# Three-token rows, PE turns for the first two blocks and a fixed instruction list in a chunked-attention plus gated-FFN kernel

## The chip, the cores and the metric

One core of one Trainium2 chip. The metric is device time in microseconds (us) of one execution. The kernel before takes 298.7 us (median of 3 runs, 298.63 to 300.44). The profile shows the span from the first to the last instruction; in every execution of which both are listed, the time is 1.7 to 2.4 us above the span. PE is TensorE (PEld its weight loads), DVE is VectorE, ACT is ScalarE, POOL is GpSimd, SP is SyncE, which issues most of the DMAs.

## The reference

Inputs are q, k, v of shape [4, 8, 768, 64], 8 memory rows per head, and three FFN weights of 512x1536, 512x1536 and 1536x512, all float32.

```python
for c in range(nc):                              # chunks of 32 queries
    l_start, r_end = max(0, 32*c - 16), min(S, 32*c + 40)
    k_full = concat([mem_k, k[:, :, l_start:r_end]], axis=2)   # v_full likewise
    scores = scale * q_c @ k_full.T
    out[chunk] = softmax(scores) @ v_full
x = out.transpose(0, 2, 1, 3).reshape(3072, 512)
y = (maximum(x @ w_gate, 0) * (x @ w_val)) @ w_out
```

## The kernel before

It works in 8 blocks of 384 tokens. A block is 4 attention steps of 96 queries (against 120 keys and 8 memory rows), 12 FFN units (four gate and four value matmuls each) and 3 output units of 12 matmuls. Attention needs q and k with the head dimension on partitions, the FFN needs the attention output x with features on partitions. All of this turning is done by DMA transposes, issued by SP.

```python
# loads: one token per partition and head, so 256 B runs
def src(self, t, h0, nh, tok, parts):
    return bass.AP(tensor=t.tensor, offset=t[self.b, h0, tok, 0].offset,
                   ap=[[D, parts], [S * D, nh], [1, D]])
...
def cast_q(self, h0, nh):            # two zero-padded copies of q, one per head of a pair
    for x in range(2):
        nc.vector.tensor_copy(self.qn[:, p0:p1, x, :, D * x:D * x + D], view[:, x])
def turn_q(self, h0, nh):
    nc.sync.dma_start_transpose(self.qT[:, p0:p1]..., self.qn[:, p0:p1]...)
...
# scores of 4 heads: two matmuls of 192 columns over 128 rows
nc.tensor.matmul(s_ps[:, i], lhsT=blk.kb[:, 2 * g + i, j, :], rhs=blk.qT[...], start=True, stop=True)
...
# start: block 0, then weights, then block 1
for h0 in (0, 4):
    b0.load_k(h0, 4, sp); b0.load_q(h0, 4, nc.scalar.dma_start); b0.load_v(h0, 4, sp)
nc.gpsimd.tensor_copy(gate, b0.qf[:, 0, 4, 0:1])
...                                  # 9 weight loads on POOL's queue, 1 MB read each
for h in range(2):
    b0.cast_k(4 * h, 4); b0.turn_k(4 * h, 4); b0.cast_q(4 * h, 4); b0.turn_q(4 * h, 4)
    b0.cast_v(4 * h, 4); b0.bands(4 * h, 4)
    if h == 0:
        load_all(blocks[1])
    ...                              # scores and values of block 0
```

The order of the program is not the order on the engines here: the framework's scheduler rearranges it.

The softmax here doesn't subtract the row's maximum and nothing guards it: scores larger than these inputs give would overflow.

Of the kernel before, what the change touches and what calls it, by code (L numbers as in the profile page):

```python
# [7 lines left out]
F32 = mybir.dt.float32  # L8
F16 = mybir.dt.float16
BF16 = mybir.dt.bfloat16  # L10
# [6 lines left out]
def kernel(  # L17
# [30 lines left out]
    KCOLS = 512  # L48
    MEMCOL = 400

    wpool = ctx.enter_context(tc.tile_pool(name="wpool", bufs=1))
    vpool = ctx.enter_context(tc.tile_pool(name="vpool", bufs=2))
    tpool = ctx.enter_context(tc.tile_pool(name="tpool", bufs=2))
    rpool = ctx.enter_context(tc.tile_pool(name="rpool", bufs=4))
    xpool = ctx.enter_context(tc.tile_pool(name="xpool", bufs=6))
# [3 lines left out]
    opool = ctx.enter_context(tc.tile_pool(name="opool", bufs=3))  # L59

    sps = ctx.enter_context(tc.tile_pool(name="sps", bufs=2, space=bass.MemoryType.PSUM))
    pps = ctx.enter_context(tc.tile_pool(name="pps", bufs=1, space=bass.MemoryType.PSUM))
    fps = ctx.enter_context(tc.tile_pool(name="fps", bufs=4, space=bass.MemoryType.PSUM))
    ops = ctx.enter_context(tc.tile_pool(name="ops", bufs=1, space=bass.MemoryType.PSUM))



    qn_t = [wpool.tile([128, HP, 2, NT, 2 * D], BF16, name=f"qn{i}") for i in range(2)]
    kf_t = [wpool.tile([128, 4, H, D], F32, name=f"kf{i}") for i in range(2)]
    vb_t = [wpool.tile([128, NJ, H, VW], F16, name=f"vb{i}") for i in range(3)]  # L70
    vf_t = [wpool.tile([128, NJ, H, D], F32, name=f"vf{i}") for i in range(2)]
    memv = wpool.tile([NMEM, B * H, D], F32, name="memv")
    ex_t = [wpool.tile([128, 4, 128], F16, name=f"ex{i}") for i in range(3)]
    for i in range(2):
        nc.vector.memset(kf_t[i][:, 3], 0.0)
    for i in range(2):
        nc.vector.memset(qn_t[i], 0.0)
    for t in vf_t:
        nc.gpsimd.memset(t[0:NMEM], 0.0)
    for t in ex_t:  # L80
        nc.gpsimd.memset(t[:, :, QB:128], 0.0)
    for t in vb_t:
        nc.gpsimd.memset(t[:, :, :, D:VW], 1.0)
# [3 lines left out]

    def build_mask(name, qb):

        m = wpool.tile([128, QB], F16, name=name)  # L90
        nc.gpsimd.memset(m, 1.0)
        bs = q_band_start(qb) - NMEM
        for g in range(QB // 32):
            c = 3 * qb + g
            lo = max(32 * c - 16, 0) - bs
            hi = min(32 * c + 40, S) - bs
            sl = m[:, 32 * g:32 * g + 32]
            if lo > NMEM:
                nc.gpsimd.affine_select(
                    out=sl, in_=sl, pattern=[[0, 32]], compare_op=ALU.is_ge,  # L100
                    fill=0.0, base=-lo, channel_multiplier=1,
                )
            if hi < 128:
                nc.gpsimd.affine_select(
                    out=sl, in_=sl, pattern=[[0, 32]], compare_op=ALU.is_ge,
                    fill=0.0, base=hi - 1, channel_multiplier=-1,
                )
        nc.gpsimd.memset(m[0:NMEM], 1.0)
        return m

    masks = {}

    def mask_of(qb):
        return masks["first" if qb == 0 else ("last" if qb == NQB - 1 else "int")]

    w_gate_sb = wpool.tile([128, NFC, DFF], F16, name="w_gate_sb")
    w_val_sb = wpool.tile([128, NFC, DFF], F16, name="w_val_sb")
    w_out_sb = wpool.tile([128, NDC, DM], F16, name="w_out_sb")

    class Block:  # L120


        def __init__(self, n):
            self.n, self.b, self.T = n, n // 2, n % 2
            self.kbase = 0 if self.T == 0 else MB - 16
            self.starts = [q_band_start(NJ * self.T + j) for j in range(NJ)]
            self.qn, self.kf = qn_t[n % 2], kf_t[n % 2]
            self.vb = vb_t[n % 3]
            self.qf = vpool.tile([128, NT, H, D], F32, name="qf")
            self.vf = vf_t[n % 2]  # L130
            self.kn = vpool.tile([128, HP, 4, 2 * D], BF16, name="kn")
            self.qT = tpool.tile([128, HP, 2, NT, 128], BF16, name="qT")
            self.kT = tpool.tile([128, HP, KCOLS], BF16, name="kT")
            self.kb = tpool.tile([128, HP, NJ, 128], BF16, name="kb")
            self.xT = None

        def src(self, t, h0, nh, tok, parts):
            return bass.AP(
                tensor=t.tensor, offset=t[self.b, h0, tok, 0].offset,
                ap=[[D, parts], [S * D, nh], [1, D]],  # L140
            )

        def load_k(self, h0, nh, dma):
            hs = slice(h0, h0 + nh)
            for t in range(3):
                dma(self.kf[:, t, hs, :], self.src(k, h0, nh, self.kbase + 128 * t, 128))  # L146
            dma(self.kf[0:16, 3, hs, :], self.src(k, h0, nh, self.kbase + 384, 16))
            dma(self.kf[16:24, 3, hs, :], bass.AP(
                tensor=mem_k.tensor, offset=mem_k[self.b, h0, 0, 0].offset,
                ap=[[D, NMEM], [NMEM * D, nh], [1, D]]))  # L150

        def load_q(self, h0, nh, dma):
            hs = slice(h0, h0 + nh)
            for t in range(NT):
                dma(self.qf[:, t, hs, :], self.src(q, h0, nh, MB * self.T + 128 * t, 128))

        def load_v(self, h0, nh, dma):
            hs = slice(h0, h0 + nh)
            for j in range(NJ):
                dma(self.vf[NMEM:128, j, hs, :], self.src(v, h0, nh, self.starts[j], BAND))  # L160

        def cast_k(self, h0, nh):
            p0, p1 = h0 // 2, (h0 + nh) // 2
            nc.vector.tensor_copy(
                self.kn[:, p0:p1], self.kf[:, :, h0:h0 + nh, :].rearrange("p t (a x) d -> p a t (x d)", x=2))

        def cast_q(self, h0, nh):
            p0, p1 = h0 // 2, (h0 + nh) // 2
            view = self.qf[:, :, h0:h0 + nh, :].rearrange("p t (a x) d -> p x a t d", x=2)
            for x in range(2):  # L170
                nc.vector.tensor_copy(self.qn[:, p0:p1, x, :, D * x:D * x + D], view[:, x])

        def cast_v(self, h0, nh):
            nc.vector.tensor_copy(self.vb[:, :, h0:h0 + nh, 0:D], self.vf[:, :, h0:h0 + nh, :])  # L174
            m = memv[:, H * self.b + h0:H * self.b + h0 + nh, :]
            m4 = bass.AP(tensor=m.tensor, offset=m.offset, ap=[m.ap[0], [0, NJ], [D, nh], [1, D]])
            nc.gpsimd.tensor_copy(self.vb[0:NMEM, :, h0:h0 + nh, 0:D], m4)  # L177

        def turn_k(self, h0, nh):
            p0, p1 = h0 // 2, (h0 + nh) // 2  # L180
            nc.sync.dma_start_transpose(  # L181
                self.kT[:, p0:p1].rearrange("p a (t c) -> p (a t) c", c=128),
                self.kn[:, p0:p1].rearrange("p a t c -> p (a t c)"))

        def turn_q(self, h0, nh):
            p0, p1 = h0 // 2, (h0 + nh) // 2
            nc.sync.dma_start_transpose(  # L187
                self.qT[:, p0:p1].rearrange("p a x t c -> p (a x t) c"),
                self.qn[:, p0:p1].rearrange("p a x t c -> p (a x t c)"))

        def bands(self, h0, nh):
            p0, np_ = h0 // 2, nh // 2
            kT, kb = self.kT, self.kb

            def band(off, mids, n):
                return bass.AP(tensor=kT.tensor, offset=kT.offset + KCOLS * p0 + off,
                               ap=[kT.ap[0], [KCOLS, np_]] + mids + [[1, n]])
            rel = [s - self.kbase for s in self.starts]
            odd = 0 if self.T == 0 else NJ - 1
            first = 1 if self.T == 0 else 0  # L200
            nc.vector.tensor_copy(kb[:, p0:p0 + np_, first:first + 3, NMEM:128],  # L201
                                  band(rel[first], [[QB, 3]], BAND))
            nc.vector.tensor_copy(kb[:, p0:p0 + np_, odd, NMEM:128], band(rel[odd], [], BAND))
            nc.vector.tensor_copy(kb[:, p0:p0 + np_, :, 0:NMEM],  # L204
                                  band(MEMCOL, [[0, NJ]], NMEM))

    n_exp = [0]

    def quad_stages(blk, j, g, x_big):
        st = {}  # L210

        def scores():
            s_ps = sps.tile([128, 2, 2, QB], F32, name="s_ps")
            for i in range(2):
                nc.tensor.matmul(  # L215
# [106 lines left out]
    for h in range(2):  # L322
# [6 lines left out]
        if h == 0:  # L329
            load_all(blocks[1])  # L330
# [61 lines left out]
```

## Time and profile before

| stretch (us) | what happens | what limits |
|---|---|---|
| 0 to 72.2 | q, k, v of blocks 0 and 1, all weights, DMA transposes, attention of blocks 0 and 1 | DMA: share 1.1 to 1.3 of 16 engines, at 176 to 198 GB/s |
| 72.2 to 290.4 | FFN of 8 blocks, attention of the next block between | PE: busy 209 of 218 us |
| 290.4 to 294.4 | last copy and store | tail |

The table of stretches of the kernel before has, for each stretch, the busy time (and instructions) of each engine, the granted clock, the DMA share and what the DMA engines moved:

```profile
core 0: us, PE busy (x) PEld busy (x) DVE busy (x) ACT busy (x) POOL busy (x), PEclk, DMA share, GB/s
0.00:22.00 22.00, 0.00 (x0) 0.00 (x0) 7.39 (x11) 1.28 (x1) 16.88 (x41) 1.00 1.11 193
22.00:45.00 23.00, 0.22 (x2) 0.32 (x3) 1.26 (x4) 0.00 (x0) 1.52 (x4) 1.00 1.27 176
45.00:72.20 27.20, 9.85 (x76) 6.22 (x75) 16.83 (x46) 6.56 (x14) 1.93 (x1) 1.00 1.09 198
```

For 45 us PE and ACT do next to nothing (POOL's 16.9 us go mostly to clearing buffers, building masks, casts and issuing weight loads), and the DMA engines are full. (The profile prints shares above 1; read them as full.) They move only 176 to 198 GB/s. The page's lines on packets and queues point to a reason, which e1 below tests:

```profile
DMA packets 146152, 45.82 MB, mean 156 GB/s; under 512 B 138436, under 2 KB 143044, under 8 KB 146132
...
q0 software_dynamic: 4800, 4.79, 9.7%
q10 hardware_dynamic: 3168, 0.79, 1.5%
```

95% of the packets are under 512 B. Queue q10 holds nothing but such packets: 1.5% of 16 engines' 294.4 us over 3168 packets is 22 ns each, or about 180 GB/s for all 16 engines. Queue q0, 9.7% of the engines' time or 28.6 us of all 16, is nearly all weights.

SP's queue shows what stands behind this traffic. Its timeline in the start (start, duration, queue, line, operation):

```profile
15.88 9.64 SPq L181 DMA_TRANSPOSE kT<-kn  x1
25.62 9.75 SPq L187 DMA_TRANSPOSE qT<-qn_94  x1
35.43 8.93 SPq L146 DMA_DIRECT2D kf_97<-in_k_dram  x3
```

The first two transposes hold SP for almost 20 us while weights and loads fill the engines, and the loads of block 1 are issued only after them. The list of PE's waits has the total, the count and the longest:

```profile
PE s_ps L215 <- DMA qT<-qn_94: 47.6, 3, 44.8
PE o_ps L231 <- DVE x_big L236: 10.7, 6, 7.4
PE s_ps L215 <- DMA qT<-qn_95: 4.6, 2, 3.8
```

The 44.8 us is the start. The other 7.4 us of waits for qT (2.8 and 4.6) lie in later blocks: PE is nearly full there, but not quite.

### The profile page before, as it was taken

What the parts mean: (1) busy time and instruction counts of PE and PEld (TensorE: products, weight loads), DVE (VectorE), ACT (ScalarE), POOL (GpSimd) and SP (SyncE); (2) the same over time, 40 slices, a digit from 0 to 9 for tenths busy, and PEclk for the clock granted to TensorE, in tenths of its full rate; (3) what the DMA queues carried; (4) which work ended last, traced back from release to release, by engine and by line L of the source; (5) the groups of instructions that cost most, each with busy time, mean ns of one, the idle gap of its engine ahead of it and who ended that gap; (6) DMA issues with size and microseconds to landing.
All of it is one profiled execution on the core that took longest, in us unless ns stands there. A gap on an engine that the chain in (4) does not pass through costs nothing.

```text
span 294.4 us, 4093 instructions
## 1 busy us (share of the span) xinstructions
PE 219.2 (74%) x1440; PEld 123.4 (42%) x1440; DVE 140.4 (48%) x355; ACT 92.9 (32%) x185; POOL 31.7 (11%) x52
## 2 busy tenths in 40 slices
PE   0000002147999799989999999999999499999983
PEld 0000001024554266546545654664565256545641
DVE  4400103675584079429924971884398127612310
ACT  1000002023342165236424622642453136423411
POOL 7950200020002000200020020002002000000000
PEclk9999999999999799999999999999999999999999
DMA  9999999997929877899499989969896611111001
GB/s 166 217 197 187 195 145 207 233 181 168 218 51 171 207 163 157 135 243 239 92 205 246 217 121 237 225 136 193 223 245 119 139 71 28 29 51 59 0 36 71
DMA packets 146152, 45.82 MB, mean 156 GB/s; under 512 B 138436, under 2 KB 143044, under 8 KB 146132
## 3 DMA queue, kind: packets, MB, share of 16 engines
q1 hardware_dynamic: 138164, 39.99, 67.1%
q0 software_dynamic: 4800, 4.79, 9.7%
q10 hardware_dynamic: 3168, 0.79, 1.5%
q8 instruction: 11, 0.18, 0.2%
q14 instruction: 9, 0.07, 0.1%
HBM read 30.34 MB, written 6.29 MB: 124 GB/s over the span
## 4 chain that ended last, share of the span: by engine, by line
PE 62%; DMA 21%; SPq 8%; DVE 5%; issue 1%; ACT 1%; ACTq 0%; DVEq 0%
PE vl_ps L273 20%; PE g_ps L269 19%; PE out_ps L284 16%; DMA vf_101<-in_v_dram 5%; DMA qT<-qn_94 5%; DMA qT<-qn_95 5%; PE o_ps L231 4%; PE s_ps L215 4%; DMA qf<-in_q_dram 3%; SPq L146 3%; DMA kf_96<-in_k_dram 2%; SPq L187 2%; SPq L181 1%; DVE gvT L277 1%; DMA xT<-x_big 1%
## 5 line engine op out<-in xcount | busy, mean ns | idle before, releaser
L269 PE MATMUL g_ps<-xT,w_gate_sb 128*128 128x384 f16 x384 | 81.9, 328 | 0.4 <-DMA xT<-x_big 0.4
L273 PE MATMUL vl_ps<-xT,w_val_sb 128*128 128x384 f16 x384 | 80.1, 329 | 0.0
L277 DVE TENSOR_TENSOR gvT<-vl_ps,g_relu 128x384 f16<-128x384 f32 x96 | 53.3, 555 | 54.3 <-PE vl_ps L273 53.0
L284 PE MATMUL out_ps<-w_out_sb,gvT 128*128 128x512 f16 x288 | 67.5, 385 | 1.6 <-ACT o_sb L287 1.3
L215 PE MATMUL s_ps<-qT,kb 128*128 128x192 bf16 x128 | 23.1, 272 | 58.4 <-DMA qT<-qn_94 47.6
L276 ACT ACTIVATE g_relu<-g_ps 128x384 f16<-128x384 f32 x96 | 47.2, 492 | 49.0 <-PE g_ps L269 31.9
L273 PEld LDWEIGHTS <-w_val_sb 128*128 128x128 f16 x384 | 37.6, 98 | 24.6 <-issue 0.7
L284 PEld LDWEIGHTS <-gvT 128*128 128x128 f16 x288 | 28.5, 99 | 36.4 <-issue 6.6
L269 PEld LDWEIGHTS <-w_gate_sb 128*128 128x128 f16 x384 | 35.7, 98 | 18.8 <-issue 1.6
L215 PEld LDWEIGHTS <-kb 128*128 128x128 bf16 x128 | 11.6, 105 | 64.4 <-DVE kb L204 40.8
L287 ACT COPY o_sb<-out_ps 128x512 f32<-128x512 f32 x24 | 14.1, 587 | 63.1 <-PE out_ps L284 63.1
L236 DVE TENSOR_TENSOR x_big<-o_ps,rinv 96x256 f16<-96x256 f32 x64 | 26.7, 418 | 1.2
L222 ACT ACTIVATE ex_104<-s_ps 128x384 f16<-128x384 f32 x22 | 10.8, 493 | 46.0 <-PE s_ps L215 44.6
L222 ACT ACTIVATE ex_105<-s_ps 128x384 f16<-128x384 f32 x21 | 10.3, 492 | 21.8 <-PE s_ps L215 20.9
L222 ACT ACTIVATE ex_106<-s_ps 128x384 f16<-128x384 f32 x21 | 10.3, 492 | 12.6 <-PE s_ps L215 11.9
L177 POOL CAST vb_99<-memv 8x2048 f16<-8x2048 f32 x3 | 5.7, 1903 | 75.9 <-DVE vb_99 L174 75.9
L177 POOL CAST vb_98<-memv 8x1024 f16<-8x1024 f32 (+1 forms) x4 | 5.8, 1458 | 64.0 <-DVE vb_98 L174 64.0
L234 DVE RECIPROCAL rinv<-o_ps 96x4 f32<-96x4 f32 x64 | 11.0, 171 | 3.2 <-PE o_ps L231 2.9
L201 DVE COPY kb<-kT 128x1440 bf16<-128x1440 bf16 (+1 forms) x9 | 4.8, 531 | 15.6 <-DMA kT<-kn 15.6
L174 DVE CAST vb_98<-vf_101 128x1024 f16<-128x1024 f32 (+1 forms) x3 | 2.6, 868 | 15.9 <-DMA vf_101<-in_v_dram 15.9
L231 PEld LDWEIGHTS <-ex_105 128*128 128x128 f16 x84 | 4.9, 103 | 11.9 <-DVE x_big L236 10.5
L177 POOL CAST vb_100<-memv 8x2048 f16<-8x2048 f32 x2 | 3.8, 1886 | 54.1 <-DVE vb_100 L174 54.1
(65 smaller groups left out, 107.6 us busy)
## 6 DMA issues: line engine op xcount, KB each, us to landing
out_dram<-o_sb SPq DMA_DIRECT2D x24, 256.0 KB
qf<-in_q_dram SPq DMA_DIRECT2D x21, 256.0 KB
vf_102<-in_v_dram SPq DMA_DIRECT2D x16, 240.0 KB
kf_97<-in_k_dram SPq DMA_DIRECT2D x12, 256.0 KB
vf_101<-in_v_dram SPq DMA_DIRECT2D x12, 240.0 KB
kf_96<-in_k_dram SPq DMA_DIRECT2D x9, 256.0 KB
w_gate_sb<-in_moe_w_gate_dram POOLq DMA_DIRECT2D x3, 512.0 KB, 10.3
w_val_sb<-in_moe_w_val_dram POOLq DMA_DIRECT2D x3, 512.0 KB, 12.7
```

Of the source, the lines that this page charges most:

```text
L177: nc.gpsimd.tensor_copy(self.vb[0:NMEM, :, h0:h0 + nh, 0:D], m4)
L215: nc.tensor.matmul(s_ps[:, i], lhsT=blk.kb[:, 2 * g + i, j, :], rhs=blk.qT[:, 2 * g + i].rearrange("p x t c -> p x (t c)")[:, :, QB * j:QB ...
L222: nc.scalar.activation(e, s_ps.rearrange("p a x c -> p (a x) c"), ACT.Exp, scale=SCALE)
L231: nc.tensor.matmul(o_ps[:, i, :], lhsT=st["ex"][:, i, :], rhs=blk.vb[:, j, 4 * g + i, :], start=True, stop=True)
L234: nc.vector.reciprocal(rinv, o_ps[0:QB, :, D:D + 1])
L236: nc.vector.tensor_tensor(out=x_big[:, 256 * g:256 * g + 256].rearrange("p (h d) -> p h d", h=4), in0=o_ps[0:QB, :, 0:D], in1=rinv_b, op=A ...
L269: nc.tensor.matmul(g_ps, lhsT=w_gate_sb[:, f, 128 * m:128 * m + 128], rhs=blk.xT[:, f, :], start=(f == 0), stop=(f == NFC - 1))
L273: nc.tensor.matmul(vl_ps, lhsT=w_val_sb[:, f, 128 * m:128 * m + 128], rhs=blk.xT[:, f, :], start=(f == 0), stop=(f == NFC - 1))
L276: nc.scalar.activation(g_relu, g_ps, ACT.Relu)
L277: nc.vector.tensor_tensor(out=state["gvT"][:, m, :], in0=vl_ps, in1=g_relu, op=ALU.mult)
L284: nc.tensor.matmul(out_ps, lhsT=state["gvT"][:, m, 128 * t:128 * t + 128], rhs=w_out_sb[:, m, :], start=(m == 0), stop=(m == NDC - 1))
L287: nc.scalar.copy(o_sb, out_ps)
```

## The change

Its intent is to get PE to the FFN sooner. For all blocks q and k, and for blocks 0 and 1 also v, are loaded with three neighbouring tokens per partition, so that a run is 768 B. Blocks 0 and 1 use no DMA transpose at all: PE turns q, k and x, and sorts keys and values into bands by matmuls with step matrices. Their instructions stand in one fixed list, and the framework's scheduler is switched off. The weight loads are spread out: POOL issues them in groups, where the kernel before issues all of them from 7.4 us on. Blocks 2 to 7 still turn by DMA, but without the zero-padded q: scores are computed on 64 rows per head. Exp runs over 8 heads at once, and the value matmuls of attention stand between an FFN unit's gate and value matmuls.

```diff
+    ctx.enter_context(tc.manual_schedule())
...
+    def load3(eng, c, n, h0=0, nh=H):
+        src = bass.AP(tensor=t.tensor, offset=t[n // 2, h0, MB * i, 0].offset,
+                      ap=[[R3 * D, 128], [S * D, nh], [1, R3 * D]])
+        eng.dma_start(dst, src)
...
+            for a in range(HP):
+                for x in range(2):
+                    r = slice(D * x, D * x + D)
...
+                        pe.matmul(o.rearrange("p (t c) -> p t c", t=R3), lhsT=self.kb[r, a, j, :],
+                                  rhs=qT_t[i][r, a, :, PP * j:PP * j + PP], start=True, stop=True)
...
+        def turn_pe(self):
+            for f in range(NFC):
+                pe.transpose(self.t16[:, f], self.x[:, 128 * f:128 * f + 128], id16[0:QB, 0:QB])
...
+    def dff(n, m, mid=()):
+        g = relu(dff_mm(n, w_gate_sb, m))
+        for f in mid:
+            f()
+        product(n, m, dff_mm(n, w_val_sb, m), g)
...
+    def gather_v(n, j):
+        mm = [(step3[:, s0 - MB * i - t:s0 - MB * i - t + BAND], v16[:, i, :, t, :]) for t in range(R3)]
...
+        for e, (w, r) in enumerate(mm):
+            pe.matmul(o[0:BAND], lhsT=w, rhs=r, start=(e == 0), stop=(e == len(mm) - 1))
...
+    def keep(n):                       # filler matmuls on zeros
+        for _ in range(n):
+            pe.matmul(PS[:, 3, 4 * VW:512], lhsT=zero[:, 0:128], rhs=zero[:, 0:512 - 4 * VW], start=True, stop=True)
...
+    load3(sp, "k", 1)
+    keep(20)
+    ORDER = """
+        kx16:A ck00:D mlast:P key0 ck01:D cq00:P key0e:A key2 key2e:A cq01:D d2 key3 vm16:D key3e:A d3 q01 q01e:A
...
+        T0 q10 kt0 kt0e:D S3 e0:A q10e:A b0:D P2 T1 x3:A M3 wb:P bm:D G4 e1:A S4 n2:D P3 bi2:D T2 G5 g4:A bi0:D
+        x4:A wc:P bi1:D n3:D S5 b3:P S6 g5:D e2:A T3 M4 P4 G6 x5:A S7 e3:D x6:A n4:D g6:A M5 M6:D fg01 P5 T4 n5:D
...
+    """.split()
...
+        elif nm == "vm16":
+            eng(vm16[:, :, :, 0:D], ...)
+            sp.dma_start(vb_t[0][BAND:128], vm16)
+            load3(sp, "q", 1)
+            load3(sp, "v", 1)
+            sp.dma_start(vb_t[1][BAND:128], vm16)
```

In the list S is scores, x exp, P value matmuls, n normalisation, T the turn of x and e its eviction, G and g the gathering of v, fg and fv gate and value matmuls of an FFN unit; the letter after the colon is the engine.

## The prediction

> **What bounds the kernel now.** Two stretches. (1) Start: in the timeline the first gate matmul runs at 72.2 us; until then PE is nearly idle, while the slice table shows the DMA engines full at only 145 to 233 GB/s. The table of queues explains the rate: nearly all packets are under 512 B (256 B rows of q, k, v), and a 250 B packet cost about 22 ns of an engine (1.5% of 16 engines' 294 us over 3168 packets), about 180 GB/s for all 16. The DMA transposes stand behind those loads: in the waits the first score matmul waits 44.8 us, for qT. (2) From 72.2 to 290.4 us PE is the limit: busy 209 of 218 us in the table of stretches. A middle block takes 26.2 us: 96 gate/value matmuls of 162 ns (four take 0.65 us in the chain), 36 output matmuls of 216 ns, together 23.4, and about 2.8 us of attention. About 9 us are PE waits, mostly for qT (pieces of 6 to 8 us in the chain). A tail of 4 us follows; the measured time is 4.3 us above the span.
>
> **What the change does.** Rows of three tokens make packets of 768 B. The Trainium skill ("DMA: Bandwidth & Descriptors", Specifications) puts line rate at 512 B and up; this trace has no 768 B packets, but its 2 KB output packets moved at about 320 GB/s (35 GB/s at a share of 0.11). I estimate 250 to 300 GB/s. Blocks 0 and 1 no longer need DMA transposes. For later blocks the zero-padded q goes (half of q's transposed bytes). PE gains about 20 us of work at the start (gathers, turns, masks), where it idled.
>
> Start, estimated: q, k, v of block 0 land by about 11 us, of block 1 by about 20. Then VectorE (about 24 us: evictions at 0.65, normalisations at 0.9, products 0.555) and ScalarE (about 22 us: exps of 768 columns at 0.78, from 492 and 587 ns; copies 0.5 to 0.6, relus 0.49) set the pace. The first FFN matmuls come at 24 to 28 us, the first eight FFN units (10.4 us of PE) are done at about 36. Then weights limit for a while: all weights cost 27 us of DMA (9.7% of the span), three blocks of q, k, v and the transposes about 33, so w_out is complete at 62 to 66 us, where a free PE would want it at 57. I put this stall, partly seen as ScalarE standing at the casts of block 2, at 5 us.
>
> Steady: 8 blocks of 23.4 = 187; attention on 6 blocks only. Scores on 64-row halves can run two at a time, saving about 0.6 us a block; the skill's "TensorEngine Tiling (Array Packing)", Key Properties, says that a mode switch drains the array, and no run shows it yet, so 2.4 us a block: 14. Small gaps 3. DMA share falls well below 0.9, so the qT waits go.
>
> Sum: FFN work as if dense from 27, stall 5, 187 + 14 + 3, tail 4 = 240 span, + 4.3: **244 us, 234 to 257**. Faster by over 2%: 0.97; within 2%: 0.02; slower: 0.01.
>
> **Right or wrong, in the profile.** First gate matmul at 24 to 28 us; packets down by more than half; steady block 25.8 us or less with no PE wait on qT; first output matmul at 62 to 66 us; PE gaps between 30 and 65 us ended by weights or block 2's loads.
>
> **What would make it wrong.** 768 B packets no better than 200 GB/s; the fixed order jamming in-order engines, so that the start passes 45 us; POOL's slow descriptor writing delaying weights; drains of a microsecond per step; or no stall at all (then 236).

## The result and the profile after

The kernel after takes 246.55 us (median of 4 runs, 245.21 to 247.25), the kernel before 298.66 beside it. The ratio is 0.8244, with a 95% interval of 0.8208 to 0.8279. A ratio here is always the mean time of one kernel's fast runs over that of the kernel before in the same rounds, so it is not quite the ratio of the medians quoted. The profiled execution has a span of 244.6 us and a granted clock of 0.996; it was a run of 246.31 us.

The stretches of the kernel after, in the same columns as above:

```profile
0.00:22.00 22.00, 17.65 (x161) 11.32 (x162) 11.29 (x27) 10.84 (x16) 14.06 (x40) 1.00 0.94 245
22.00:38.00 16.00, 14.71 (x182) 9.54 (x181) 10.24 (x26) 10.45 (x19) 8.21 (x14) 1.00 0.97 163
38.00:67.30 29.30, 29.06 (x222) 17.14 (x220) 16.32 (x32) 15.17 (x29) 6.77 (x12) 1.00 1.06 181
```

PE, idle for 45 us before, is now busy nearly from the beginning (its first 5 us are filler). From 22 us on it is busy 14.7 of 16 us, then 29.1 of 29.3 us. The packet lines of the page after:

```profile
DMA packets 84414, 39.46 MB, mean 161 GB/s; under 512 B 57112, under 2 KB 81432, under 8 KB 84392
```

Packets fell by 42%, not by more than half: v of blocks 2 to 7 is still loaded in rows of 256 B (by the shapes of these loads about 23,000 of the 57,112 small packets that are left). PE's timeline gives the milestones:

```profile
30.23 0.82 PE L307 MATMUL PS<-xT,w_gate_sb 128*128 128x384 f16 x4
...
43.85 0.81 PE L307 MATMUL PS<-xT,w_gate_sb 128*128 128x384 f16 x4
...
67.26 1.89 PE L334 MATMUL PS<-w_out_sb,gvT 128*128 128x512 f16 x8
69.69 1.02 PE L334 MATMUL PS<-w_out_sb,gvT 128*128 128x512 f16 x4 [0.55 <-DMA w_out_sb<-in_moe_w_out_dram]
...
84.82 0.81 PE L307 MATMUL PS<-xT,w_gate_sb 128*128 128x384 f16 x4 [0.90 <-DMA xT<-x_big]
...
87.77 0.81 PE L307 MATMUL PS<-xT,w_val_sb 128*128 128x384 f16 x4 [0.84 <-ACT o_sb L348]
```

The first gate matmul runs at 30.2 us instead of 72.2: 42 of the span's 49.8 us. The remaining 8 us are about the size of the 7.4 us of qT waits in later blocks, and PE's list of waits no longer has a wait for qT at all; no run separates the parts of these 8 us. At 43.85 us the first eight FFN units (64 matmuls) are done. Between there and 90 us only three waits over 0.3 us are left, 2.3 us together: for w_out, for xT and for an output buffer.

A middle block did not get shorter. The chain of waits after shows the beginnings of the output units of blocks 4 and 5, 26.17 us apart, as before (26.2):

```profile
156.71 7.77 PE PS L334 x36
...
182.88 7.77 PE PS L334 x36
```

### The profile page after: what moved, and what is told of

It is laid out like the page before. It is cut to its first block, busy times and chain, and to the rows that moved or that the text cites. A ratio compares the mean times of both kernels' runs of the same rounds, so it can differ in the third digit from the quotient of the medians.

```text
span 244.6 us, 4600 instructions
## 1 busy us (share of the span) xinstructions
PE 231.6 (95%) x1751; PEld 129.6 (53%) x1751; DVE 112.4 (46%) x233; ACT 114.4 (47%) x199; POOL 47.8 (20%) x102
## 2 busy tenths in 40 slices
DMA packets 84414, 39.46 MB, mean 161 GB/s; under 512 B 57112, under 2 KB 81432, under 8 KB 84392
## 4 chain that ended last, share of the span: by engine, by line
PE 74%; DMA 12%; SPq 7%; DVE 3%; issue 1%; ACT 1%; POOL 1%; ACTq 0%; DVEq 0%
PE PS L307 45%; PE PS L334 19%; DMA qraw<-in_q_dram 5%; DMA w_out_sb<-in_moe_w_out_dram 4%; PE PS L277 3%; SPq L170 3%; PE PS L260 2%; DMA vraw<-in_v_dram 1%; DVE x_big L286 1%; DMA out_dram<-o_sb 1%; PE PS L405 1%; SPq L169 1%; PE PS L295 1%; DVE qn L177 1%; SPq L191 1%
## 5 line engine op out<-in xcount | busy, mean ns | idle before, releaser
L307 PE MATMUL PS<-xT,w_gate_sb 128*128 128x384 f16 x384 | 77.9, 327 | 0.9 <-DMA xT<-x_big 0.9
L307 PE MATMUL PS<-xT,w_val_sb 128*128 128x384 f16 x384 | 77.5, 326 | 0.8 <-ACT o_sb L348 0.8
L321 DVE TENSOR_TENSOR gvT<-PS,g_relu 128x384 f16<-128x384 f32 x72 | 39.9, 554 | 81.9 <-PE PS L307 65.5
L312 ACT ACTIVATE g_relu<-PS 128x384 f16<-128x384 f32 x96 | 47.0, 491 | 51.6 <-PE PS L307 29.5
L334 PE MATMUL PS<-w_out_sb,gvT 128*128 128x512 f16 x288 | 63.6, 379 | 0.6 <-DMA w_out_sb<-in_moe_w_out_dram 0.6
L307 PEld LDWEIGHTS <-w_gate_sb 128*128 128x128 f16 x384 | 35.4, 98 | 25.4 <-issue 1.4
L334 PEld LDWEIGHTS <-gvT 128*128 128x128 f16 x288 | 27.7, 98 | 32.9 <-issue 0.8
L213 POOL COPY kb<-kT 128x480 f16<-128x480 f16 (+1 forms) x18 | 13.7, 856 | 112.7 <-DMA kT<-kn 112.7
L348 ACT COPY o_sb<-PS 128x512 f32<-128x512 f32 x23 | 13.5, 585 | 47.4 <-PE PS L334 41.0
L266 ACT ACTIVATE ex<-PS 128x768 f16<-128x768 f32 x32 | 25.9, 811 | 8.5 <-PE PS L260 7.4
L286 DVE TENSOR_TENSOR x_big<-PS,rinv 96x512 f16<-96x512 f32 x32 | 22.0, 687 | 1.1
L319 DVE TENSOR_TENSOR gvT<-PS,g_relu 128x384 f16<-128x384 f32 x24 | 13.2, 553 | 12.4 <-PE PS L307 12.3
L277 PE MATMUL PS<-vb,ex 128*128 128x66 f16 x256 | 13.4, 194 | 0.6 <-ACT xT L298 0.2
## 6 DMA issues: line engine op xcount, KB each, us to landing
w_val_sb<-in_moe_w_val_dram POOLq DMA_DIRECT2D x2, 512.0 KB, 10.7
```

Of the source, the lines that this page charges most:

```text
L213: eng(dst(1, r, [[128, nj], [R3, 40]]), src(kT, TS * t + P + (r > 0), [[PP, nj], [1, 40]]))
L266: act.activation(self.ex[:, :, 0:QB].rearrange("p (h b) c -> p b h c", b=2), PS[:, self.sb:self.sb + 2, 0:HP * QB].rearrange("p b (h c) -> ...
L277: pe.matmul(PS[:, 2 + h // 4, VW * (h % 4):VW * (h % 4) + VW], lhsT=self.ex[:, h, :], rhs=self.vb[:, self.j, h, :], start=True, stop=True)
L286: dve.tensor_tensor(out=self.x.rearrange("p (b h d) -> p b h d", b=2, h=4), in0=o[:, :, :, 0:D], in1=rb, op=ALU.mult)
L307: pe.matmul(o, lhsT=w_sb[:, f, 128 * m:128 * m + 128], rhs=xTs[n][:, f], start=(f == 0), stop=(f == NFC - 1))
L312: act.activation(g_relu, g_ps, ACT.Relu)
```

## The experiments

Twelve kernels ran besides the two. All gave the right result. One of e11's six runs was slow and is left out of its ratio. Times of different experiments come from several chips, so small differences are judged by the ratio to the kernel before of the same rounds (after: 0.8244) and by milestones in the trace. "After" below means the changed kernel.

### What the start pays for: packet size

e1 cuts each three-token load into three loads of one token per partition and head.

```diff
-        eng.dma_start(dst, src)
+        for t_ in range(R3):        # dst: [:, i, h0:h0 + nh, t_]; source token MB * i + t_, runs of D
+            eng.dma_start(d_, s_)
```

> The same kernel as after, but each three-token load is cut into three loads of one token per partition and head, so its packets are 256 B again (nothing else moves). Theory A (the start waits for q, k, v, and packet size sets how fast they come: in the chain 5.8 us for q of block 0 and 6.3 us for q of block 1): a tensor of 3072 packets at about 22 ns over 16 engines takes 4.3 us instead of about 2.5, six tensors before the FFN, so the first gate matmul moves from 30.2 us to 36 to 40 us, the first output matmul from 67.3 to 73 to 78, the time to 253 to 259 us. Rival B (the gain is the turning on PE, packets do not matter): within 1.5 us of 246.6.

Measured: 258.43 us, ratio 0.8655 (0.8571 to 0.8739). The first gate matmul came at 37.2 us, the first output matmul at 75.6: theory A, inside its ranges. The stretches of e1 and then of after, in the same columns:

```profile
10.00:20.00 10.00, 7.37 (x71) 4.21 (x69) 4.21 (x6) 5.50 (x9) 2.55 (x4) 1.00 1.09 219
20.00:30.00 10.00, 7.00 (x79) 5.16 (x80) 5.43 (x12) 3.97 (x6) 4.30 (x7) 0.66 0.93 158
```

```profile
10.00:20.00 10.00, 8.75 (x98) 5.39 (x99) 6.43 (x10) 6.36 (x11) 5.52 (x7) 1.00 1.07 287
```

With full engines the 256 B packets moved 219 GB/s where the 768 B packets moved 287. Two impurities: e1 issues 18 more DMAs in the start at about 0.5 us of SP each, and its granted clock reads 0.66 between 20 and 30 us (0.50 from 24 to 28), where "after" has 1.00. So 12 us (4.1 points of the ratio times 299) is the whole effect of the shorter runs, and not of the transfer rate alone.

### What the start pays for: DMA transposes

e2 turns x of blocks 0 and 1 by DMA again.

```diff
-            st[r[0]].turn_pe()
+            st[r[0]].turn_dma()
         elif c == "e":
-            st[r[0]].turned(eng)
+            pass
```

> The same as after, but the attention output x of blocks 0 and 1 is turned by DMA as before and not by PE (32 PE transposes and 8 evictions less). Theory A (DMA transposes queue behind loads and weights in a start with full DMA engines, several us each): the first gate matmul gets later by 3 to 8 us, time 249 to 255. Rival B (a DMA transpose is no worse when PE is the limit, and PE loses about 1.4 us of work): 245 to 247.

Measured: 252.51 us, ratio 0.8463 (0.8389 to 0.8537): theory A. The first gate matmul came at 37.7 us. The transposes in SP's queue (shortest, middle and longest ns, first and last start), a piece of the chain of waits, and the wait on PE:

```profile
L290 SPq DMA_TRANSPOSE xT<-x_big x8: 1180/1191/1617, 20.3 to 45.9; - x8
```

```profile
26.78 10.68 DMA xT<-x_big
```

```profile
37.71 1.44 PE L307 MATMUL PS<-xT,w_gate_sb 128*128 128x384 f16 x4 [8.70 <-DMA xT<-x_big]
```

Each transpose holds SP for only about 1.2 us. But the last one of block 0, issued at 26.8 us, lands 10.7 us later beside the weight loads, and PE waits 8.7 us for it. The attention that stands behind this wait in PE's order comes late too, so the last three transposes are issued only at 40 to 46 us, and the loads of block 2 behind them at 47.2 us instead of 33.0. The first four gate matmuls take 1.44 us instead of 0.82; the granted clock reads 0.50 there.

### Would a better order have done it without PE?

The rival explanation of the 42 us is that in the kernel before the weights come too early. Three attempts move them in the kernel before; two of them failed as tests.

```diff
-    gate = wpool.tile([128, 1], F32, name="gate")          # e5: the gate reads v of block 1,
-    nc.gpsimd.tensor_copy(gate, b0.qf[:, 0, 4, 0:1])       # after load_all(blocks[1])
+        nc.gpsimd.tensor_copy(dst[32:33, 0, c:c + 1], late) # e12: written into each weight tile
+    late = blocks[1].vf[32:33, 3, 0, 0:1]                  # e9: rows 0:1, which no load writes
```

> The kernel before, with one thing moved: its weight loads start only when the last v load of block 1 has landed, instead of at 7.3 us. Theory C (in the kernel before it is the 27 us of weight traffic among the q, k, v loads and transposes that delays the start, and ordering alone would have won much of the gain): first gate matmul from 72.2 us to 50 to 60 us, time 277 to 288. Theory A (packet size and DMA turns are what the start pays for, and the weights' bytes must be moved before the FFN in any order): first gate matmul at 66 to 76 us, time 293 to 303.

Measured: 298.08 us, ratio 0.9948 (0.9879 to 1.0017), first gate matmul at 70.9 us. It tested nothing: the scheduler issued the weight loads at 13.3 us, ahead of the gate that should have held them.

> The run e5 did not test what it should: the gate was only an order on paper, and the trace shows the weight loads issued at 13.3 us, long before the gate ran at 55.4 us. Here each weight tile has one element written from the last v load of block 1 before its load, a data dependence, so no weight moves before block 1 is loaded. Theory C (ordering alone would have won much of the gain): blocks 0 and 1 need about 29 us of loads (20,400 packets at 22.5 ns over 16 engines) and about 12 us of transposes, the first weights 6 us more; first gate matmul at 50 to 58 us, time 278 to 288. Theory A (packet size and DMA turns are the cost, whatever the order): first gate matmul at 65 to 76 us, time 292 to 303.

Measured: 298.63 us, ratio 1.0000 (0.9954 to 1.0046). This failed too: the element came from a row of the v tile that the load does not write, so the weights went at 17.3 us. Even so, block 0's first scores now ran before 20 us instead of at 44.8, and the first gate matmul still came at 72.5 us.

> The run e9 failed as a test too: the element came from a row of the v tile that the load does not write, so the weights were held to 17.3 us only. Here it comes from a row that the last v load of block 1 writes, and the weight loads stand after block 0's attention in the program. Theory C (with the weights out of the way, ordering alone wins much of the gain): blocks 0 and 1 loaded and turned by about 41 us (about 29 us of loads, 12 of transposes), first weights 6 us later, first gate matmul at 48 to 58 us, time 278 to 290. Theory A (order does not help, the packets and the turns themselves are the cost): first gate matmul at 65 us or later, time 292 or more. If the first gate matmul comes early but the time does not fall, the weights' 27 us were only moved to where PE waits for them.

Measured: 306.02 us, ratio 1.0271 (1.0187 to 1.0354): slower, though whether by 2% is not clear. Here the weights did wait: v of block 1 had landed at 30.2 us, and the first weight load was issued at 32.5. The first gate matmul came at 70.1 us: theory A for this order. The chain of waits of e12 shows why:

```profile
25.88 4.27 DMA vf<-in_v_dram
30.27 1.11 DVE vb L174
31.38 2.98 DMA kT<-kn
34.37 25.44 DMA qT<-qn
...
62.41 4.31 SPq L255
66.82 3.13 DMA xT<-x_big
70.08 1.44 PE g_ps L269 x4
```

All of q, k, v is there at 30 us. But the last transpose of q, issued at 34.4 us beside the weights, lands 25.4 us later; the transposes of x follow it in SP's queue. With the weights first the loads and transposes stand behind them; with the weights last the remaining transposes do. The weights are on POOL's queue and the transposes on SP's, and it does not help. The Trainium skill says as much ("DMA: Bandwidth & Descriptors", Issuing engines are not separate DMA queues): DMAs of all issuing engines run on the same 16 DMA engines and interleave. This trace fits, at 195 GB/s and a share of 1.22 between 40 and 60 us. Turning on PE takes the transposes out of this traffic. What e12 does not show is that no order can: it issues all nine weight loads within 10 us, beside the last turn of q and ahead of all turns of x. An order that holds the weights until these turns have landed, or that spreads them out as the new kernel does, was not run in the kernel before.

### Who sets the pace of the new start?

e3 adds 18 filler matmuls to PE, e4 three copies to VectorE, both at about 27 us and without data dependence.

```diff
-    S6 g5:D
+    S6 d9 d9 g5:D              # e3
+    S6 zz:D zz:D zz:D g5:D     # e4: zz is a copy of 128x1024 float32
```

> The same as after, with 18 more filler matmuls of 248 columns on PE (about 1.9 us of PE) at about 27 us, no data dependence. Theory A (from about 22 us on the start is one dense PE stream, PE sets the pace): all of it shows in the first output matmul, 67.3 to 69.2 us; the 0.55 us wait for w_out goes, so the time rises by 0.9 to 1.9 us. Rival B (my prediction: VectorE and ScalarE set the pace of the start and PE has slack): less than 0.4 us.

> The same as after, with three more copies of 128x1024 float32 on VectorE (about 0.7 us each, 2 us together) at the same point of the order, no data dependence on the rest. Theory A (PE sets the pace): at most 0.7 us more, from the wait of one step. Rival B (VectorE sets the pace): about 2 us more.

The first gate matmul itself moves between runs: e6, e7 and e8 below, whose list differs from that of "after" only well before or well behind this point, have it 0.2 to 0.8 us earlier. The mark to count from is therefore the start of the scores just ahead of the fill. The lines in PE's timelines of after and e3, and in those of PE and VectorE of e4:

```profile
27.40 0.39 PE L257 MATMUL PS<-qp,kb 64*128 64x96 f16 x10
```

```profile
26.82 0.39 PE L257 MATMUL PS<-qp,kb 64*128 64x96 f16 x10
...
28.18 2.08 PE L424 MATMUL PS<-zero 128*128 128x248 f16 x18
```

```profile
27.95 0.39 PE L258 MATMUL PS<-qp,kb 64*128 64x96 f16 x10
28.18 2.46 DVE L484 COPY scr<-scr 128x1024 f32<-128x1024 f32 x3
```

| | added | scores ahead of the fill | first gate matmul | between the two | first output matmul | ratio |
|---|---|---|---|---|---|---|
| after | | 27.40 | 30.23 | 2.83 | 67.3 | 0.8244 (0.8208 to 0.8279) |
| e6, e7, e8 | | 27.20, 26.60, 26.69 | 30.04, 29.44, 29.53 | 2.84 each | 66.8, 68.2, 67.6 | below |
| e3, PE | 1.9 us | 26.82 | 31.57 | 4.75 | 68.3 | 0.8259 (0.8191 to 0.8327) |
| e4, VectorE | 2.5 us | 27.95 | 31.57 | 3.62 | 68.5 | 0.8298 (0.8221 to 0.8375) |

From the mark to the first gate matmul, all 1.9 us of PE's fill show (4.75 against 2.83), but only 0.8 of VectorE's 2.5 us (3.62). Of these 0.8 us PE spends 0.35 waiting for VectorE's eviction of x, and 0.35 waiting longer for POOL's copy of the bands, which took 1.01 us beside the copies instead of 0.65. That is theory A in both runs: PE sets the pace here, and VectorE has 1.7 us of slack at this point. e4 was already 0.6 us late before its copies began, e3 0.6 us early; taken alone, their equal 31.57 us would mislead. In the time both effects are inside the noise. (The copies took 0.82 us each, not the 0.7 expected.) Slack of ScalarE was not tested.

e6 leaves out all 33 filler matmuls.

```diff
-        for _ in range(n):
+        for _ in range(0):
```

> The same as after without the 33 filler matmuls on zeros (5 us of PE time in the start). Theory A (they hold the PE clock up: in the kernel before the first scores after the idle start took 0.80 us per four, 0.5 later, and the first gate matmuls 1.44 us per four, later 0.81): the attention matmuls of the start run slow until about 20 us, first gate matmul 31.5 to 34, time +1 to +4. Rival B (they only cost PE time in a start that PE limits): first gate matmul 0 to 1.5 us earlier, time -1 to 0.

Measured: 245.53 us, ratio 0.8200 (0.8159 to 0.8242), first gate matmul at 30.0 us, first output matmul at 66.8: rival B. The clock did matter where A said it would. PE's timeline of e6, and then of after, for the same six key matmuls:

```profile
8.27 1.38 PE L368 MATMUL PS<-step,kn 128*128 128x360 f16 x6 [1.73 <-DVE kn L177]
```

```profile
7.42 0.79 PE L368 MATMUL PS<-step,kn 128*128 128x360 f16 x6 [0.51 <-DVE kn L177]
```

This fits the state that the Trainium skill describes ("TensorE: Matmul & The Clock Gate", Part 1: a default half-rate clock, released after about 3.4 us of sustained activity); in e6 it lasted longer, through 5.6 us of dense work from 8.3 to 13.9 us. The profile's granted clock does not show it: it reads 1.00 for e6 between 5 and 21.7 us, although in e2 it does read 0.50 between 34 and 42 us. Until 14 us the matmuls of e6 are slow, but after spends time on fillers and on a wait of 0.64 us for q of block 1 at 19.3 us, so e6 has caught up at 22 us. The fillers buy nothing here.

### Scores on half the rows

e7 issues the eight score matmuls of a step as four on one half of the rows and four on the other, instead of alternating, in blocks 2 to 7.

```diff
-            for a in range(HP):
-                for x in range(2):
+            for x in range(2):           # blocks 2 to 7 only
+                for a in range(HP):
```

> The same as after, but in blocks 2 to 7 the eight score matmuls of a step are issued as four on the upper 64 rows and then four on the lower, instead of alternating. Theory A (neighbours on different halves run at the same time, and switching between 64 and 128 rows costs about 0.2 us a step, which is why the step still takes 0.37 us with its switches): eight in a row then cost 8 x 0.04, so a step grows by 0.15 to 0.2 us, 24 steps by 3.6 to 4.8 us, time 250 to 251.5. Rival B (they never overlapped: 8 x 0.04 is already 0.33 and the switch costs next to nothing): time 246 to 247, score steps 0.27 us as before.

The time, 247.69 us (ratio 0.8297, 0.8247 to 0.8347), is a little up, but not by the steps themselves. PE's timeline of e7, then of after, around one step:

```profile
175.77 0.81 PE L308 MATMUL PS<-xT,w_val_sb 128*128 128x384 f16 x4
176.51 0.35 PE L261 MATMUL PS<-qT,kb 64*128 64x96 f16 x8
176.80 0.82 PE L308 MATMUL PS<-xT,w_gate_sb 128*128 128x384 f16 x4
```

```profile
178.33 0.81 PE L307 MATMUL PS<-xT,w_val_sb 128*128 128x384 f16 x4
179.07 0.34 PE L260 MATMUL PS<-qT,kb 64*128 64x96 f16 x8
179.35 0.82 PE L307 MATMUL PS<-xT,w_gate_sb 128*128 128x384 f16 x4
```

The four value matmuls take 0.65 us from start to start, so the step begins 0.09 us after they have been fed, and from their end to the next gate matmul it takes 0.38 us in e7 and 0.37 in after. In the kernel before, the same work as four matmuls of 192 columns took 0.33 us. Rival B is right about the steps: alternating halves saves 0.01 us, although the time lies above its 246 to 247. (What holds each step at this length, the array or the separate weight load of each of the eight matmuls, is not tested.) 8 x 96 columns in 0.28 us is little less than the 0.33 us that they took in the kernel before, and the 0.09 us at the switch takes it back. The rest of e7's time is waits elsewhere: 1.1 us for w_out instead of 0.55, and 2.0 us for bands of k that POOL had not finished.

### Attempts at a better version

e8 issues v of block 3 two units later and has six output buffers, e10 issues q and v of block 1 right behind k, e11 joins both, drops the fillers and turns k of later blocks two units earlier.

```diff
+        if u == 18:                                   # e8; the loads stood under u == 16
             for j in range(NJ): load_v(3, j)
     load3(sp, "k", 1)
+    load3(sp, "q", 1)                                 # e10, and gone from behind vm16
+    load3(sp, "v", 1)
+                if u == 10:                           # e11; the turn stood under u == 12
                     turn_k(n + 2)
```

> The same as after, with the eight v loads of block 3 issued two units later (after the last turn of x of block 2 is in the SyncE queue) and six output buffers instead of three. Theory A (the 0.9 us wait for xT and the 0.84 us wait for o_sb near 84 us come from SyncE's queue standing in those loads): both waits go, time -1 to -2 us (244.5 to 245.5). Rival B (the waits come from full DMA engines, and move): within 0.5 us of 246.6.

Measured: 245.35 us, ratio 0.8203 (0.8161 to 0.8245). Theory A in the trace: the FFN of block 2 begins at 83.8 us instead of 84.8, with no wait for xT or o_sb. (Two things were changed at once; which of them removed which wait is not separated.) PE's waits for the bands of k, which POOL makes, grew from 0.2 to 1.9 us (1.3 us ahead of block 2's first scores, at 57.6 us, and 0.6 us at 168.2 us) and take part of it back; in the time the gain of 1.2 us is not clear of noise.

> The same as after, but q and v of block 1 are issued right behind k of block 1 (at about 8 us) instead of behind the cast of the memory rows and its copy (12.4 us), for which SyncE's queue stood 3.8 us. Theory A (arrival of q and v of block 1, at 18.7 and 21.2 us, holds the start): q lands 1.5 to 3 us earlier, first gate matmul 0.8 to 2 us earlier (28.2 to 29.4), but the weights move with the same engines, so w_out lands when it did and the wait for it grows to 1.2 to 2.5 us: time -0.8 to +0.3. Rival B (with PE and VectorE both nearly full from 22 us on, arrival does not matter): first gate matmul within 0.4 us of 30.2.

Measured: 250.11 us, ratio 0.8382 (0.8343 to 0.8421): slower than after, and neither theory. PE's timeline of e10 shows a wait that I had not thought of:

```profile
20.68 0.41 PE L277 MATMUL PS<-vb,ex 128*128 128x66 f16 x8 [2.13 <-DMA vb<-vm]
```

The memory rows of v (33 KB), which the first value matmuls need, now stand behind q and v of block 1 (1.6 MB): issued at 12.8 us, they land at 20.6. The first gate matmul came at 35.0 us, 4.7 later than in after. The wait of 2.1 us is not all of this: in this execution, the slowest of the four, the granted clock reads 0.50 from 22 to 28 us. e11 below has the same late memory rows at a clock of 1.00, and its first gate matmul comes at 32.4. What looked like SP standing idle for a cast was a small urgent transfer kept ahead of large ones.

> An attempt at a better version: after with q and v of block 1 issued early (as e10), no filler matmuls (as e6), v of block 3 issued late and six output buffers (as e8), and in blocks 2 to 5 the DMA turn of k issued two units earlier, which should take away the wait for the bands that cost e7 and e8 1 to 2 us. Expected if these gains add: no wait for xT, o_sb or the bands, 243 to 244.8 us, 0.7 to 1.4% under after. If the wait for w_out takes the start's share back: 244.5 to 245.5.

Measured: 246.52 us (245.49 without its slow run), ratio 0.8242 (0.8201 to 0.8284), the same as after; the expected gain did not come. The later part improved as planned (no wait for xT, o_sb, w_out or the later bands), and the start lost part of what e10 lost: PE waits 1.4 us for the memory rows, and the first gate matmul comes at 32.4 us. No version clearly beats the change.

## Why the prediction was right or wrong

The range held: 244 us predicted, 246.55 measured. The sum did not hold term by term, and that the total came so close is partly luck: the start (6.8 us) and attention (2.6) cost more than predicted, and the stall, the gaps and the time above the span 7.8 us less. "Start" is the time at which the FFN would have begun had PE run it without a gap: the first output matmul at 67.3 us, less 192 gate and value matmuls of 0.1625 us (31.2) and block 2's attention until then (2.3).

| term (us) | predicted | measured |
|---|---|---|
| start, FFN as if dense | 27 | 33.8 |
| stall for supply | 5 | 2.3 (0.55 + 0.90 + 0.84) |
| FFN matmuls | 187 | 187 |
| attention of six blocks | 14 | 16.6 (2.8 a block; block 2 takes 2.6) |
| small gaps | 3 | 0.5 (what is left) |
| tail | 4 | 4.4 |
| time above span | 4.3 | 1.7 |

- **Mechanism of the start: right.** Larger packets and no DMA turns for blocks 0 and 1. q, k, v came as estimated (287 GB/s; the last v of block 1 at 21.2 us against "about 20"), and e1 and e2 each put back one part: about 12 and 6 us of time, 7.0 and 7.5 us at the first gate matmul. The rule that the prediction took from the skill ("DMA: Bandwidth & Descriptors", Specifications: line rate needs transfers of 512 B or more) fits 287 against 219 GB/s in its direction; whether 287 is the line rate no run shows. The two runs together put back 18 of the 52 us. The rest (q and k turned on PE, the gathering of bands, the spread-out weights, the fixed list) was never taken out by itself, and of the other orders only that of e12 was tested.
- **Size of the start: the step that failed.** "Then VectorE ... and ScalarE ... set the pace", with PE's 20 us of extra work "where it idled", and the first eight FFN units "done at about 36" us; they were done at 43.9. The FFN and the early attention share PE. In e6, without fillers, PE works 29.3 us between 5.0 and 38.3 us, of which 33 FFN matmuls are 5.4: 23.9 us are attention work, and from 21.7 us on PE idles only 1.3 of 16.6 us. (About 2 of the 23.9 us are there only because the first matmuls of e6 run slow.) The first FFN units could not hide behind VectorE. VectorE and ScalarE were sized about right (22.0 and 21.3 us busy until 38.5 us in after, against 24 and 22), but PE sets the pace: of work added at 28 us, all of PE's 1.9 us reach the first gate matmul and 0.8 of VectorE's 2.5 us (e3, e4). PE had to be added up.
- **Stall: wrong in size and kind.** "w_out is complete at 62 to 66 us, where a free PE would want it at 57". It was complete at 69.7 us; PE began on it at 67.3 and wanted the last third at 69.1. PE came 10 us later than predicted and w_out 4 to 8 us later, so the stall nearly vanished. No PE gap between 30 and 65 us was ended by weights or by block 2's loads.
- **Attention: wrong.** "Scores on 64-row halves can run two at a time, saving about 0.6 us a block". They saved nothing (e7), so a middle block stayed at 26.2 us instead of 25.8 or less. The skill's drain at a switch ("TensorEngine Tiling (Array Packing)", Key Properties) fits the 0.09 us ahead of each step, which is an upper bound for the switch into a step; the switch back cannot be told apart from the matmuls.
- **Later blocks: right.** No PE wait on qT, and a DMA share of 0.69 to 0.84 between 100 and 190 us instead of 0.78 to 0.99. Which part did it is not shown: e1 raises the share to 0.95 to 1.02 there and still has no such wait, so the lower share alone is not the cause. The bytes of the unpadded q and the place of the turns in the order stay open.
- **Time above the span: a slip.** I took the span of one execution (294.4 us) from the median time of others (298.7). Executions with both numbers show 1.7 to 2.4 us. This error of 2.6 us hid half of the span's miss (240 against 244.6).
- **Packets "down by more than half": wrong**, 42%; I had forgotten that v of later blocks keeps its 256 B rows.

Not tested: the exp over 8 heads (0.811 us instead of two of 0.492) and the place of the value matmuls. ScalarE is not the limit in a middle block, so I argue, without a run, that they are worth little.

## What to carry to other kernels

When the start of a kernel is full of DMA, take work off the DMA engines (longer runs, turns on an idle PE); the one reordering that was tested only changed who waits, and a transpose beside bulk loads can wait long (25 us in e12, 10.7 in e2). When idle-time work is moved to the engine that will be the bottleneck, add up that engine too: its first useful work starts only when the moved work is done. Before a transfer is moved to the front, look for the small transfers that it will push back. When two runs differ before the point that was changed, count from a mark just ahead of it (e3, e4).

## What the Trainium skill lacked or had wrong

- "DMA: Bandwidth & Descriptors", Latency and other measured facts: gives a DMA transpose an effective 261 GB/s or more, and no page gives its rate beside bulk traffic. In e12 one transpose of q (24 x 128 rows of 256 B, 0.79 MB) took 25.4 us from issue to landing, 31 GB/s, beside the weight loads; in e2 one of 0.1 MB took 10.7 us.
- "TensorE: Matmul & The Clock Gate", Part 3, Measured speedup vs the span model: the speedups of row tiling are for 512 columns. At 64 rows and 96 columns, two tiles, the runs show none, with separate weights for each matmul: a step took 0.37 us alternating, 0.38 us unpaired, and 0.33 us as zero-padded 128-row matmuls.
- "TensorEngine Tiling (Array Packing)", Key Properties: no size is given for the drain at a mode switch. Here the switch into 64-row matmuls takes at most 0.09 us.
- "TensorE: Matmul & The Clock Gate", Part 4: about 275 ns for a 128x128 transpose in context, and no spacing of several in a row. Here one takes 219 ns, and in a row they overlap: after's six transposes of q at 22.07 us were followed by six of k at 22.40 us, 55 ns each.
